# Relu² attention with a Fourier-mix feed-forward: mirrored rows stored by one indirect scatter, 112-row stores, DFT tables and first weights moved to the start

## The chip, the core and the metric

The kernel runs on one NeuronCore of a Trainium2 chip. TensorE (PE) does the matmuls and transposes, VectorE (DVE), ScalarE (ACT) and GpSimd (POOL) the elementwise work; PE's weight loads stand as PEld. SyncE (SP) issues the transfers that store and reload rows, and POOL those that load and cast the inputs. Each engine works through its own instructions in a fixed order; semaphores tie them together. The metric is device time in microseconds, lower is better.

## The reference

```python
# q, k, v: [8, 12, 448, 64] f32; w1: [768, 3072]; w2: [3072, 768]
scores = q @ k^T / 8
attn   = max(scores, 0)**2 / 448
x = heads joined: (attn @ v) -> [8, 448, 768]
mixed = real(fft(fft(x, axis=1), axis=2))
u  = x + mixed
un = (u - mean(u)) / sqrt(var(u) + 1e-6)         # over the last axis
out = u + max(un @ w1, 0) @ w2
```

## The kernel before

A pass runs once for each of the 8 batches, and three of them overlap. `attention(b)` makes for each pair of heads the scores (L374, PE), their relu (L406, ACT), its square (L400, DVE) and the product with v (L388, PE). `mix(b)` applies the two DFTs as matmuls with cosine and sine tables (`chan`, L555, and `seq`, L471), forms `u = x + mixed` and its normalised form `un` (L516, DVE), and turns `un` by PE (L598) into `unT`, which ACT copies out of PSUM (L602). `ffns` takes 384 tokens for an even batch and 512 for an odd one (its own 448 and the 64 left over), multiplies by w1 (L653), applies relu (L643, ACT), then for each chunk of 128 tokens and each half of the 768 columns multiplies by w2 (L688); DVE adds the product to the residual rows `o` (L670).

The DFT of a real sequence is symmetric, so `mix` computes tokens 0 to 224 and their mirror images 447 to 225 from the same products. It does so in two row pieces `ch`, and each makes two tiles: `us[0]` with tokens s (added on DVE, L491 and L492) and `us[1]` with tokens 448 - s (added on POOL, same lines). The residual rows wait in DRAM: `mix_store` writes `us[0]` to `usc` (L527), writes `us[1]`, whose rows stand in reverse order, to a second DRAM buffer `ubo` (L534), and when that has landed copies `ubo` to `usc` with the rows reversed (L537). The pieces have 113 and 112 rows; the four stores have 113, 112, 112 and 111 rows, and the copies are written as 2 x 112 x 384 and 2 x 111 x 384. `reload` later brings 128 rows of `usc` into one of two tiles `o` (L634); the tile is free again when the store of the finished chunk (L675) has landed.

All of L527, L534, L537, L634 and L675 are issued by SP, one after the other, and each may wait for a semaphore first. All input loads (q, k and v of a group of four heads, L252; w1 in two halves, L266; w2, L276) are issued by POOL and share its queue. The order is made by a planner in the kernel: generators yield the engine, a duration and what must be done first, and `Streams.run` emits the step that can start earliest; ties go by rank. `loading` lists the loads: batch 0, first half of w1, batch 1, second half of w1, w2, batch 2 and on. `build_dft` makes the tables: index rows by POOL (iota), angles on DVE (dfty and dftr, L195 to L231), sines on ACT (L199).

Of the kernel before, what the change touches and what calls it, by code (L numbers as in the profile page):

```python
# [9 lines left out]
FP32 = mybir.dt.float32  # L10
BF16 = mybir.dt.bfloat16
AF = mybir.ActivationFunctionType
ALU = mybir.AluOpType
# [101 lines left out]
def kernel(  # L115
# [9 lines left out]
    nc = tc.nc  # L125
# [10 lines left out]
    KN = D // 2 + 1  # L136
    HG = 4
    NG = H // HG
    SC = [(0, R1), (R1, NS)]
    XB = 2  # L140

    const = ctx.enter_context(tc.tile_pool(name="const", bufs=1))
# [2 lines left out]
    psum = ctx.enter_context(tc.psum_pool(name="ps", bufs=1))  # L145
    dram = ctx.enter_context(tc.tile_pool(name="dr", bufs=1, space=bass.MemoryType.DRAM))

    usc = dram.tile([B * S, D], FP32, name="usc")
    ubo = dram.tile([B * S, D], FP32, name="ubo")

    def psS():
        return psum.tile([128, 2, 512], FP32, name="psS", tag="S", bufs=2)
# [14 lines left out]
    eps_t = const.tile([128, 1], FP32, name="eps_t")  # L167
    ident = const.tile([128, 128], BF16, name="ident")

    rev = const.tile([128, R1], BF16, name="rev")  # L170
    qT_bufs = []

    def constants():
        make_identity(nc, ident)
        nc.gpsimd.memset(zero_t, 0.0)
        nc.gpsimd.memset(eps_t, 1e-6)
        for i in range(3):
            t = const.tile([128, NQ], BF16, name=f"qT{i}")
            nc.gpsimd.memset(t[:, NS:NS + 1], 0.0)
            nc.gpsimd.memset(t[:, NQ - 1:NQ], 0.0)  # L180
            qT_bufs.append(t)
        nc.gpsimd.memset(rev, 0.0)
        nc.gpsimd.affine_select(out=rev, in_=rev, compare_op=ALU.not_equal, fill=1.0, base=-R,
                                pattern=[[1, R1]], channel_multiplier=1)

    seq = const.tile([R1, 2, 2, NS], BF16, name="seqm")
    chan = [const.tile([128, 2, 2 * KH], BF16, name=f"chan{m}") for m in range(3)]
    dft_ready = Cell()

    def build_dft():  # L190
        def sincos(dst, y, n, p):

            e = yield need("DVE", n / 1920 + n / 960 + 0.3)
            r = work.tile([128, 4 * KH], FP32, name="dftr", tag="o", bufs=2)
            nc.vector.tensor_scalar(r[:p, :n], y[:p, :n], float(2 ** 23), float(2 ** 23),  # L195
                                    op0=ALU.add, op1=ALU.subtract)
            nc.vector.tensor_tensor(y[:p, :n], y[:p, :n], r[:p, :n], op=ALU.subtract)
            e = yield need("ACT", act(n), [e + LATENCY["DVE"]])
            nc.scalar.activation(dst, y[:p, :n], AF.Sin, bias=zero_t[:p], scale=2.0 * math.pi)  # L199
            dft_ready.t = e + LATENCY["ACT"]  # L200

        e = yield need("POOL", 1.4)
        row = const.tile([128, 8], FP32, name="drow")
        col = work.tile([128, 2 * KH], FP32, name="dcol", tag="tm", bufs=1)
        col2 = work.tile([128, 2 * KH], FP32, name="dcol2", tag="tp", bufs=1)
        nc.gpsimd.iota(row[:, 0:2], pattern=[[R1, 2]], base=0, channel_multiplier=1,
                       allow_small_or_imprecise_dtypes=True)
        nc.gpsimd.iota(row[:, 4:7], pattern=[[128, 3]], base=0, channel_multiplier=1,
                       allow_small_or_imprecise_dtypes=True)
        nc.gpsimd.iota(col[:, 0:NS], pattern=[[1, NS]], base=0, channel_multiplier=0,  # L210
                       allow_small_or_imprecise_dtypes=True)
        nc.gpsimd.iota(col2, pattern=[[1, 2], [2, KH]], base=0, channel_multiplier=0,
                       allow_small_or_imprecise_dtypes=True)
        e = yield need("DVE", 0.16, [e + LATENCY["POOL"]])
# [30 lines left out]
    def load_group(i):  # L245

        b, g = divmod(i, NG)
        hs = slice(g * HG, (g + 1) * HG)
        for x, (nm, src) in enumerate((("q", q), ("k", k), ("v", v))):
            e = yield need("POOL", 0.85, bufs=[BQ[x]])  # L250
            t = work.tile([R, 2 * HG, 2 * Dh], BF16, name=f"{nm}n", tag=f"{nm}n", bufs=3)
            nc.gpsimd.dma_start(  # L252
                out=t, in_=src[b, hs].rearrange("h (f p j) d -> p (h f) (j d)", f=2, j=2))
            loads[i][x] = t.rearrange("p (h f) (j d) -> p (f j) h d", f=2, j=2)
            ready[i][x].t = sch.dma(e, GRP)

    w1_sb = [[None] * 2 for _ in range(MC)]
    w2_sb = [None] * 4
# [22 lines left out]
    def loading():  # L281
        for i in range(NG):
            yield from load_group(i)
        yield from load_w1(0)
        for i in range(NG, 2 * NG):
            yield from load_group(i)
        yield from load_w1(1)
        yield from load_w2()
        for i in range(2 * NG, B * NG):
            yield from load_group(i)  # L290
# [231 lines left out]
    def mix_store(b, ch, us, ut, freed):  # L522
        s0, s1 = SC[ch]
        n = s1 - s0
        r0 = b * S
        e = yield need("SP", 0.1, [ut[0]])
        nc.sync.dma_start(out=usc[r0 + s0:r0 + s1, :], in_=us[0][:n])  # L527
        st0 = sch.dma(e, n * D * 4)
        u_stored[b][2 * ch].t = st0

        lo, hi = (1, R1) if ch == 0 else (0, n - 1)
        t0 = r0 + S - s0 - (hi - 1)
        e = yield need("SP", 0.1, [ut[1]])
        nc.sync.dma_start(out=ubo[t0:t0 + hi - lo, :], in_=us[1][lo:hi])  # L534
        st1 = sch.dma(e, n * D * 4)
        e = yield need("SP", 0.1, [st1] + freed)
        nc.sync.dma_start(  # L537
            out=usc[t0:t0 + hi - lo, :].rearrange("t (a d) -> a t d", a=2)[:, ::-1, :],
            in_=ubo[t0:t0 + hi - lo, :].rearrange("t (a d) -> a t d", a=2))
        u_stored[b][2 * ch + 1].t = sch.dma(e, n * D * 4)  # L540
        BU[0].free.append(max(st0, freed[0].t))
        BU[1].free.append(max(st1, freed[1].t))

    def mix(b):
# [44 lines left out]
        for m2 in range(3):  # L589
            e1 = yield need("PE", 8 * 0.06, un_ready[b], [BS])  # L590
            pu = psS()
            for h in range(2):
                ms = slice((2 * m2 + h) * 128, (2 * m2 + h + 1) * 128)
                for t, n, idn, c0, w in ((0, R1, ident[:R1, :R1], 0, R1),
                                         (2, R, ident[:R, :R], R1, R),
                                         (3, R, rev[:R, 2:R1], NS, R - 1),
                                         (1, R1, rev[:R1, 0:R], NS + R - 1, R)):
                    nc.tensor.matmul(pu[:, h, c0:c0 + w], lhsT=uns[b][t][:n, ms], rhs=idn,  # L598
                                     start=True, stop=True)
# [17 lines left out]
    def ffns():  # L617
        for b in range(B):
# [9 lines left out]
            def reload():  # L628
                c = len(os)
                if c < NC:  # L630
                    stored = u_stored[b] + (u_stored[b - 1] if b % 2 else [])
                    e = yield need("SP", 0.1, stored, [BO])
                    o = work.tile([128, D], FP32, name="o", tag="o", bufs=2)
                    nc.sync.dma_start(out=o, in_=usc[T0 + c * 128:T0 + (c + 1) * 128, :])  # L634
                    os.append((o, sch.dma(e, 128 * D * 4)))

            pend = None
# [60 lines left out]

    LEAD = 1.6
    with tc.manual_schedule():  # L700
        constants()
        sch.engine.update(POOL=1.8)

        sch.add(loading(), (0, 4))
        sch.add(build_dft(), (0, 9))
        sch.add(turning(), (2, 2))
        sch.add(ffns(), (4, 0))
        sch.add(mixes(), (1, 1))
# [32 lines left out]
```

## Time and profile before

| | |
|---|---|
| median of 3 runs | 796.37 us (796.13 to 797.03) |
| the profiled execution | 797.58 us; its span from first to last instruction 795.8 us |
| PE busy | 668.2 us, 84% of the span |
| DVE, ACT, POOL busy | 385.7, 357.6, 105.7 us |
| chain that ended last: waits on `o<-usc` and on `out_dram<-o` | 12% and 7% of the span |
| stores and mirror copies of the residual rows | 16 + 16 + 16 transfers of 333 to 339 KB |

All rows used below are of that one execution. A row of the timeline gives start, duration, engine, line, operation and tiles; the bracket at its end gives how long the engine had been idle and what it had waited for. A row of the windows gives, for one stretch, each engine's busy time with its count of instructions, then the granted TensorE clock (1.00 is full), the mean busy share of the 16 DMA engines, and GB/s. Line numbers are those of the kernel before; the changed kernel's own lines are named where its order is shown.

### The profile page before, as it was taken

To read this page: it belongs to the slowest core of one execution; us is meant where nothing else is said; L and a number is where in the kernel's file an instruction comes from. 1 tells how busy PE (TensorE), PEld (TensorE's weight loads), DVE (VectorE), ACT (ScalarE), POOL (GpSimd) and SP (SyncE) were. 2 spreads that over 40 slices of the span, in tenths; PEclk is the share of its full clock that TensorE was granted. 3 is DMA by queue.
4 is the path that set the end of the run, shared out by engine and by line. 5 is a ranking of instruction groups with operands and counts; after the bars stand their busy time and mean duration, and the time that the engine had idled before them with its cause. 6 is when DMAs were issued, how large, how long until landed. Compare 5 with 4: busy or idle time off the path is not lost.

```text
span 795.8 us, 10685 instructions
## 1 busy us (share of the span) xinstructions
PE 668.2 (84%) x4270; PEld 361.1 (45%) x4288; DVE 385.7 (48%) x894; ACT 357.6 (45%) x557; POOL 105.7 (13%) x144
## 2 busy tenths in 40 slices
PE   4774905996999769996999769996999779996998
PEld 2232402563446435563446444563446444563454
DVE  3987503484445635375454735375454644370001
ACT  3773713533664236533665136534565146522410
POOL 7134101120112111120112111120111100020000
PEclk9997766997999889997999988998999989998999
DMA  9959922622634255322634253332631232012212
GB/s 142 139 59 210 226 50 63 68 66 75 119 35 56 80 127 103 33 71 75 119 36 55 76 129 90 36 66 88 122 39 22 71 114 70 1 50 95 80 40 79
DMA packets 86114, 65.15 MB, mean 82 GB/s; under 512 B 67136, under 2 KB 73776, under 8 KB 86064
## 3 DMA queue, kind: packets, MB, share of 16 engines
q0 software_dynamic: 70528, 25.96, 27.6%
q1 hardware_dynamic: 15536, 38.52, 14.2%
q8 instruction: 33, 0.54, 0.3%
q14 instruction: 17, 0.14, 0.1%
HBM read 68.40 MB, written 27.50 MB: 121 GB/s over the span
## 4 chain that ended last, share of the span: by engine, by line
PE 55%; DMA 20%; DVE 13%; another core or an unknown queue 4%; ACT 3%; issue 2%; POOL 2%; SPq 0%; DVEq 0%; ACTq 0%; POOLq 0%
PE psF L653 28%; DMA o<-usc 12%; PE psF L688 11%; DMA out_dram<-o 7%; PE psT L388 5%; PE psS L374 4%; DVE sq L400 2%; PE psT L325 2%; PE psS L555 2%; DVE stats L502 2%; ACT rsc L406 1%; DVE o L670 1%; DMA w<-in_moe_w_ch_dram 1%; DVE un L516 1%
## 5 line engine op out<-in xcount | busy, mean ns | idle before, releaser
L406 ACT ACTIVATE rsc<-psS 112x900 bf16<-112x900 f32 x192 | 174.4, 920 | 216.4 <-DVE sq L400 122.1
L653 PE MATMUL psF<-unT,w 128*128 128x384 bf16 (+1 forms) x1134 | 236.8, 359 | 2.3 <-ACT hT L643 0.7
L688 PE MATMUL psF<-w,hT 128*128 128x384 bf16 x1344 | 237.8, 332 | 0.0
L688 PEld LDWEIGHTS <-hT 128*128 128x128 bf16 x1344 | 128.9, 99 | 95.8 <-issue 19.7
L653 PEld LDWEIGHTS <-w 128*128 128x128 bf16 x1152 | 109.0, 99 | 118.4 <-issue 30.7
L643 ACT ACTIVATE hT<-psF 128x384 bf16<-128x384 f32 (+1 forms) x192 | 104.3, 545 | 67.3 <-PE psF L653 67.0
L400 DVE TENSOR_TENSOR sq<-rsc 112x900 bf16<-112x900 bf16 x192 | 114.3, 620 | 40.7 <-ACT rsc L406 33.3
L670 DVE TENSOR_TENSOR o<-psF,o 128x384 f32<-128x384 f32 x56 | 30.7, 548 | 151.3 <-DMA o<-usc 82.2
L374 PE MATMUL psS<-qT,kT 64*112 64x450 bf16 x384 | 71.5, 433 | 15.0 <-ACT rsc L406 7.3
L252 POOL DMA_DIRECT2D vn<-in_v_dram x24 | 19.9, 828 | 415.5 <-PE psT L388 405.0
L388 PE MATMUL psT<-sq,vn 112*64 112x450 bf16 x384 | 65.9, 413 | 5.2 <-DVE sq L400 4.3
L414 DVE TENSOR_SCALAR xT<-psT 128x450 bf16<-128x450 f32 x48 | 30.0, 624 | 81.3 <-PE psT L388 81.1
L325 PE MATMUL psT<-ident,qkr 112*128 112x112 bf16 x336 | 28.9, 240 | 45.3 <-DVE xT L414 43.7
L325 PEld LDWEIGHTS <-qkr 112*128 112x128 bf16 x384 | 28.5, 116 | 64.0 <-DVE qkr L315 34.1
L598 PE MATMUL psS<-ident,un 113*128 113x113 bf16 x96 | 16.9, 283 | 36.2 <-ACT rsc L406 36.2
L374 PEld LDWEIGHTS <-kT 64*112 64x112 bf16 x384 | 23.1, 137 | 53.1 <-issue 45.8
L332 DVE COPY qT<-psT 128x224 bf16<-128x224 bf16 x42 | 16.4, 391 | 49.5 <-PE psT L325 49.3
L598 PEld LDWEIGHTS <-un 113*128 113x128 bf16 x192 | 17.8, 138 | 47.7 <-DVE qkr L315 37.5
L388 PEld LDWEIGHTS <-vn 112*64 112x64 bf16 x384 | 17.2, 114 | 43.3 <-issue 42.8
L491 POOL TENSOR_TENSOR u<-tp,xn 113x385 f32<-113x385 f32 (+1 forms) x16 | 14.9, 929 | 158.8 <-issue 96.0
L502 DVE BATCH_NORM_STATS2 stats<-u 113x6 f32<-113x384 f32 (+1 forms) x64 | 31.7, 535 | 0.7 <-POOL u L491 0.4
L602 ACT ACTIVATE unT<-psS 128x768 bf16<-128x768 f32 (+1 forms) x24 | 20.5, 868 | 20.3 <-PE psS L598 20.3
(71 smaller groups left out, 478.8 us busy)
## 6 DMA issues: line engine op xcount, KB each, us to landing
o<-usc SPq DMA_DIRECT2D x28, 384.0 KB
out_dram<-o SPq DMA_DIRECT2D x28, 384.0 KB
qn<-in_q_dram POOLq DMA_DIRECT2D x24, 224.0 KB, 5.5
kn<-in_k_dram POOLq DMA_DIRECT2D x24, 224.0 KB, 5.9
vn<-in_v_dram POOLq DMA_DIRECT2D x24, 224.0 KB, 4.4
w<-in_moe_w_ch_dram POOLq DMA_DIRECT2D x12, 384.0 KB, 11.4
w<-in_moe_w_ch_dram POOLq DMA_DIRECT2D x4, 1152.0 KB, 38.9
usc<-u SPq DMA_DIRECT2D x8, 339.0 KB
```

The lines of the kernel that those rows point to most:

```text
L325: nc.tensor.transpose(pt[:, x * S + c * R:x * S + (c + 1) * R], qk[x][:, c, hs], ident[:R, :R])
L374: nc.tensor.matmul(sc[:R, h, 0:NQ], lhsT=kT[ps, c * R:(c + 1) * R], rhs=qT[ps, :], start=True, stop=True)
L388: nc.tensor.matmul(av[h * Dh:(h + 1) * Dh, 0:NQ], lhsT=vn[:, c, h0 + h, :], rhs=sq[:, h, :], start=(c == 0), stop=(c == 3))
L400: nc.vector.tensor_tensor(sq, r, r, op=ALU.mult)
L406: nc.scalar.activation(r, sc[:R, :, 0:NQ], AF.Relu)
L414: nc.vector.tensor_scalar(x, av[:, 0:NQ], 1.0 / (64.0 * S), None, op0=ALU.mult)
L502: nc.vector.bn_stats(stats[:n, hf, :], u[:n, hf * (D // 2):(hf + 1) * (D // 2)])
L598: nc.tensor.matmul(pu[:, h, c0:c0 + w], lhsT=uns[b][t][:n, ms], rhs=idn, start=True, stop=True)
L643: nc.scalar.activation(h[:, 0:N], ph[:, 0:N], AF.Relu)
L653: nc.tensor.matmul(ph[:, 0:N], lhsT=w1_sb[m][hf][:, jj * 128:(jj + 1) * 128], rhs=unT[:, m, 0:N], start=(m == 0), stop=(m == MC - 1))
L670: nc.vector.tensor_tensor(o[:, hs], pc[:, 0:D // 2], o[:, hs], op=ALU.add)
L688: nc.tensor.matmul(pc[:, 0:D // 2], lhsT=hT[j][:, c * 128:(c + 1) * 128], rhs=w2_sb[j // 6][:, j % 6, hs], start=(j == 0), stop=(j == JC - 1))
```

## The change

1. The DRAM buffers `usc` and `ubo` become two tensors for each batch, `utop` (224 rows) and `ubot` (225 rows). The row pieces become 112 and 113 rows. SP stores 112 rows of `us[0]` for each piece, and for the second piece the one row left over goes to `ubot`. `us[1]` is written to `ubot` by one indirect DMA on POOL's queue: a column of row numbers (`back`) gives each partition its destination row, so the rows land already reversed. The copies of L537 and the buffer between are gone. A reload that crosses a tensor's border becomes two or three transfers.
2. The index rows for the DFT tables, `ident` and `rev` are made by POOL between the first loads, small memsets go to DVE, and `build_dft` gets the rank (0, 3) for (0, 9).
3. The second half of w1 is loaded before batch 1; w2 comes after batch 1.

```diff
-    SC = [(0, R1), (R1, NS)]
+    SC = [(0, R), (R, NS)]
-    usc = dram.tile([B * S, D], FP32, name="usc")
-    ubo = dram.tile([B * S, D], FP32, name="ubo")
+    HS = S // 2
+    utop = [dram.tile([HS, D], FP32, name=f"utop{b}") for b in range(B)]
+    ubot = [dram.tile([HS + 1, D], FP32, name=f"ubot{b}") for b in range(B)]
...
+        for i in range(2):
+            nc.gpsimd.iota(back[i], pattern=[[0, 1]], base=(2 - i) * R, channel_multiplier=-1)
...
+            if i == 0 and x == 1:
+                e = yield need("POOL", 1.0)
+                dft_indices()
+                indices_ready.t = e + LATENCY["POOL"]
...
         yield from load_w1(0)
+        yield from load_w1(1)
         for i in range(NG, 2 * NG):
             yield from load_group(i)
-        yield from load_w1(1)
         yield from load_w2()
...
         e = yield need("SP", 0.1, [ut[0]])
-        nc.sync.dma_start(out=usc[r0 + s0:r0 + s1, :], in_=us[0][:n])
+        nc.sync.dma_start(out=utop[b][s0:s0 + R, :], in_=us[0][:R])
+        if ch == 1:
+            nc.sync.dma_start(out=ubot[b][0:1, :], in_=us[0][R:R1])
...
-        e = yield need("SP", 0.1, [ut[1]])
-        nc.sync.dma_start(out=ubo[t0:t0 + hi - lo, :], in_=us[1][lo:hi])
+        e = yield need("POOL", 1.2, [ut[1]])
+        nc.gpsimd.indirect_dma_start(
+            out=ubot[b], out_offset=bass.IndirectOffsetOnAxis(ap=back[ch], axis=0),
+            in_=us[1][:R], in_offset=None)
-        e = yield need("SP", 0.1, [st1] + freed)
-        nc.sync.dma_start(
-            out=usc[t0:t0 + hi - lo, :].rearrange("t (a d) -> a t d", a=2)[:, ::-1, :],
-            in_=ubo[t0:t0 + hi - lo, :].rearrange("t (a d) -> a t d", a=2))
...
-        sch.add(build_dft(), (0, 9))
+        sch.add(build_dft(), (0, 3))
```

What SP issues around the mix of batch 2, while the second feed-forward group runs; before, `u` rows go out by four stores and two copies:

```order
L527 DMA usc_69<-u_2519 113x768
L534 DMA ubo_70<-u_2516 112x768
L634 DMA o_2535<-usc_69 128x768
L537 DMA usc_69<-ubo_70 2x112x384
L527 DMA usc_69<-u_2604 112x768
L534 DMA ubo_70<-u_2586 111x768
L675 DMA out_0_dram<-o_2157 128x768
L634 DMA o_2649<-usc_69 128x768
L537 DMA usc_69<-ubo_70 2x111x384
```

Now the same place on SP; the one-row store L548 waits until the first piece's scatter has landed, because both write `ubot`, and the second piece's scatter (L553, on POOL) waits in turn for that row:

```order
L546 DMA utop2_71<-u_2537 112x768
L658 DMA o_2553<-utop1_70 32x768
L658 DMA o_2553<-ubot1_78 96x768
L546 DMA utop2_71<-u_2623 112x768
L548 DMA ubot2_79<-u_2623 1x768
L700 DMA out_0_dram<-o_2175 128x768
L658 DMA o_2668<-ubot1_78 128x768
L700 DMA out_0_dram<-o_2553 128x768
```

The two copies and the two stores to `ubo` have left SP's row; the reload of the last chunk (o_2668) is behind one chunk store alone.

The loads in POOL's row, before, from the third group of batch 1 to the first piece of w2 (`w1_m_h` is row block m, half h):

```order
L252 DMA qn_469<-in_q_dram 112x8x128
L252 DMA kn_476<-in_k_dram 112x8x128
L252 DMA vn_588<-in_v_dram 112x8x128
L266 DMA w1_0_1_595<-in_moe_w_ch1_dram 128x1536
L266 DMA w1_1_1_597<-in_moe_w_ch1_dram 128x1536
L266 DMA w1_2_1_612<-in_moe_w_ch1_dram 128x1536
L266 DMA w1_3_1_635<-in_moe_w_ch1_dram 128x1536
L266 DMA w1_4_1_642<-in_moe_w_ch1_dram 128x1536
L266 DMA w1_5_1_659<-in_moe_w_ch1_dram 128x1536
L276 DMA w2_0_674<-in_moe_w_ch2_dram 128x6x768
```

And now, from the end of w1 to the first piece of w2:

```order
L286 DMA w1_4_1_278<-in_moe_w_ch1_dram 128x1536
L286 DMA w1_5_1_280<-in_moe_w_ch1_dram 128x1536
L262 DMA qn_296<-in_q_dram 112x8x128
L262 DMA kn_305<-in_k_dram 112x8x128
L262 DMA vn_380<-in_v_dram 112x8x128
L262 DMA qn_393<-in_q_dram 112x8x128
L262 DMA kn_399<-in_k_dram 112x8x128
L262 DMA vn_499<-in_v_dram 112x8x128
L262 DMA qn_506<-in_q_dram 112x8x128
L262 DMA kn_511<-in_k_dram 112x8x128
L262 DMA vn_618<-in_v_dram 112x8x128
L296 DMA w2_0_625<-in_moe_w_ch2_dram 128x6x768
```

All twelve pieces of w1 now stand ahead of batch 1's nine loads, where six of them stood behind these.

DVE's first instructions before go straight to the copies of q and k; the tables came in between the squares from the 26th instruction on. Now two tables' angles stand around the first copies:

```order
L225 TENSOR_SCALAR drow_91<-drow_91 128x2
L226 TENSOR_SCALAR drow_91<-drow_91 128x3
L232 TENSOR_SCALAR dfty_123<-dcol_92,drow_91 113x225 x2
L216 TENSOR_SCALAR dftr_130<-dfty_123 113x450
L218 TENSOR_TENSOR dfty_123<-dfty_123,dftr_130 113x450
L335 COPY qkr_135<-qn_111 112x1024
L232 TENSOR_SCALAR dfty_138<-dcol_92,drow_91 113x225 x2
L335 COPY qkr_143<-kn_113 112x1024
L216 TENSOR_SCALAR dftr_145<-dfty_138 113x450
L218 TENSOR_TENSOR dfty_138<-dfty_138,dftr_145 113x450
```

The work on the tables moved from the middle of batch 0's attention to its start; PE's own order changes by a few swaps in batch 0 alone.

More of the change, by code (lines that the diff above doesn't have):

```diff
@@ L168 @@
     ident = const.tile([128, 128], BF16, name="ident")
-    rev = const.tile([128, R1], BF16, name="rev")
+    rev = const.tile([128, R], BF16, name="rev")
+    back = [const.tile([R, 1], mybir.dt.int32, name=f"back{i}") for i in range(2)]
     qT_bufs = []
[L173 to L176, printed above, removed]
+    drow = const.tile([128, 8], FP32, name="drow")
+    dcol = work.tile([128, 2 * KH], FP32, name="dcol", tag="tm", bufs=1)
@@ new lines, with dft_indices @@
+    dcol2 = work.tile([128, 2 * KH], FP32, name="dcol2", tag="tp", bufs=1)
+    def dft_indices():
+        nc.gpsimd.iota(drow[:, 0:2], pattern=[[R, 2]], base=0, channel_multiplier=1,
+                       allow_small_or_imprecise_dtypes=True)
+        nc.gpsimd.iota(drow[:, 4:7], pattern=[[128, 3]], base=0, channel_multiplier=1,
+                       allow_small_or_imprecise_dtypes=True)
+        nc.gpsimd.iota(dcol[:, 0:NS], pattern=[[1, NS]], base=0, channel_multiplier=0,
+                       allow_small_or_imprecise_dtypes=True)
+        nc.gpsimd.iota(dcol2, pattern=[[1, 2], [2, KH]], base=0, channel_multiplier=0,
+                       allow_small_or_imprecise_dtypes=True)
@@ L177, in constants, with small_constants, mirrors @@
+    def small_constants():
+        nc.vector.memset(zero_t, 0.0)
+        nc.vector.memset(eps_t, 1e-6)
         for i in range(3):
             t = const.tile([128, NQ], BF16, name=f"qT{i}")
-            nc.gpsimd.memset(t[:, NS:NS + 1], 0.0)
-            nc.gpsimd.memset(t[:, NQ - 1:NQ], 0.0)
+            nc.vector.memset(t[:, NS:NS + 1], 0.0)
+            nc.vector.memset(t[:, NQ - 1:NQ], 0.0)
             qT_bufs.append(t)
+    def mirrors():
         nc.gpsimd.memset(rev, 0.0)
-        nc.gpsimd.affine_select(out=rev, in_=rev, compare_op=ALU.not_equal, fill=1.0, base=-R,
-                                pattern=[[1, R1]], channel_multiplier=1)
+        nc.gpsimd.affine_select(out=rev, in_=rev, compare_op=ALU.not_equal, fill=1.0,
+                                base=1 - R, pattern=[[1, R]], channel_multiplier=1)
+        for i in range(2):
+            nc.gpsimd.iota(back[i], pattern=[[0, 1]], base=(2 - i) * R, channel_multiplier=-1)
@@ L186 @@
     seq = const.tile([R1, 2, 2, NS], BF16, name="seqm")
     chan = [const.tile([128, 2, 2 * KH], BF16, name=f"chan{m}") for m in range(3)]
-    dft_ready = Cell()
+    dft_ready, indices_ready = Cell(), Cell()
     def build_dft():
@@ L200, in sincos @@
             dft_ready.t = e + LATENCY["ACT"]
[L202 to L214, printed above, removed]
+        row, col, col2 = drow, dcol, dcol2
+        e = yield need("DVE", 0.16, [indices_ready])
         nc.vector.tensor_scalar(row[:, 0:2], row[:, 0:2], 1.0 / S, None, op0=ALU.mult)
@@ L255, in load_group @@
             ready[i][x].t = sch.dma(e, GRP)
+            if i == 0 and x == 1:
+                e = yield need("POOL", 1.0)
+                dft_indices()
+                indices_ready.t = e + LATENCY["POOL"]
+            if i == 0 and x == 2:
+                yield need("POOL", 0.7)
+                make_identity(nc, ident)
+            if i == 1 and x == 2:
+                yield need("POOL", 0.7)
+                mirrors()
     w1_sb = [[None] * 2 for _ in range(MC)]
@@ L524, in mix_store @@
         n = s1 - s0
-        r0 = b * S
         e = yield need("SP", 0.1, [ut[0]])
-        nc.sync.dma_start(out=usc[r0 + s0:r0 + s1, :], in_=us[0][:n])
+        nc.sync.dma_start(out=utop[b][s0:s0 + R, :], in_=us[0][:R])
+        if ch == 1:
+            nc.sync.dma_start(out=ubot[b][0:1, :], in_=us[0][R:R1])
         st0 = sch.dma(e, n * D * 4)
         u_stored[b][2 * ch].t = st0
-        lo, hi = (1, R1) if ch == 0 else (0, n - 1)
-        t0 = r0 + S - s0 - (hi - 1)
-        e = yield need("SP", 0.1, [ut[1]])
-        nc.sync.dma_start(out=ubo[t0:t0 + hi - lo, :], in_=us[1][lo:hi])
+        e = yield need("POOL", 1.2, [ut[1]])
+        nc.gpsimd.indirect_dma_start(
+            out=ubot[b], out_offset=bass.IndirectOffsetOnAxis(ap=back[ch], axis=0),
+            in_=us[1][:R], in_offset=None)
         st1 = sch.dma(e, n * D * 4)
-        e = yield need("SP", 0.1, [st1] + freed)
-        nc.sync.dma_start(
-            out=usc[t0:t0 + hi - lo, :].rearrange("t (a d) -> a t d", a=2)[:, ::-1, :],
-            in_=ubo[t0:t0 + hi - lo, :].rearrange("t (a d) -> a t d", a=2))
-        u_stored[b][2 * ch + 1].t = sch.dma(e, n * D * 4)
+        u_stored[b][2 * ch + 1].t = st1
+        e = yield need("SP", 0.0, freed)
         BU[0].free.append(max(st0, freed[0].t))
@@ L593, in mix @@
                 ms = slice((2 * m2 + h) * 128, (2 * m2 + h + 1) * 128)
[L594 to L597, printed above, removed]
+                for t, n, idn, c0, w in ((0, R, ident[:R, :R], 0, R),
+                                         (2, R1, ident[:R1, :R1], R, R1),
+                                         (3, R, rev[:R, :], NS, R),
+                                         (1, R, rev[:R, 0:R - 1], NS + R, R - 1)):
                     nc.tensor.matmul(pu[:, h, c0:c0 + w], lhsT=uns[b][t][:n, ms], rhs=idn,
@@ L633, in reload @@
                     o = work.tile([128, D], FP32, name="o", tag="o", bufs=2)
-                    nc.sync.dma_start(out=o, in_=usc[T0 + c * 128:T0 + (c + 1) * 128, :])
+                    r0, end = T0 + c * 128, T0 + (c + 1) * 128
+                    t = r0
+                    while t < end:
+                        bb, r = divmod(t, S)
+                        src, r = (utop[bb], r) if r < HS else (ubot[bb], r - HS)
+                        w = min(HS - r, end - t)
+                        nc.sync.dma_start(out=o[t - r0:t - r0 + w, :], in_=src[r:r + w, :])
+                        t += w
                     os.append((o, sch.dma(e, 128 * D * 4)))
@@ L700 @@
     with tc.manual_schedule():
-        constants()
-        sch.engine.update(POOL=1.8)
+        small_constants()
+        sch.engine.update(POOL=0.5, DVE=0.8)
         sch.add(loading(), (0, 4))
-        sch.add(build_dft(), (0, 9))
+        sch.add(build_dft(), (0, 3))
         sch.add(turning(), (2, 2))
```

## The prediction

> **What bounds the kernel now.** I read the page's slices first, then the waits, then the timeline at the longest waits, then windows over them for the DMA engines and the clock.
>
> ```profile
> span 795.8 us, 10685 instructions
> PE   4774905996999769996999769996999779996998
> PEclk9997766997999889997999988998999989998999
> ```
>
> PE is at 9 in most slices; one early slice reads 0, and every few slices there is a dip to 6 or 7, each time with a lower clock. The waits from 130 us to the end (time, times, longest) name what PE and DVE stood for:
>
> ```profile
> DVE o L670 <- DMA o<-usc: 82.2, 10, 12.9
> PE psS L598 <- ACT rsc L406: 35.6, 6, 6.4
> PE psT L325 <- DVE xT L414: 17.0, 3, 6.4
> PE psS L598 <- DVE un L516: 7.5, 1, 7.5
> ```
>
> Ten waits of DVE for a reload, and 6 + 3 + 1 = 10 waits of PE, 35.6 + 17.0 + 7.5 = 60.1 us. They are the same ten places. Two of them, on DVE and PE, and SP's issues around them:
>
> ```profile
> 274.02 0.56 DVE L670 TENSOR_TENSOR o<-psF,o 128x384 f32<-128x384 f32 x1 [5.77 <-DMA o<-usc]
> 276.79 0.35 PE L598 MATMUL psS<-ident,un 113*128 113x113 bf16 x2 [5.46 <-ACT rsc L406]
> 293.30 0.56 DVE L670 TENSOR_TENSOR o<-psF,o 128x384 f32<-128x384 f32 x1 [12.39 <-DMA o<-usc]
> 295.52 0.90 PE L325 MATMUL psT<-ident,qkr 112*128 112x112 bf16 x8 [6.12 <-DVE xT L414]
> ```
>
> ```profile
> 254.18 0.34 SPq L675 DMA_DIRECT2D out_dram<-o  x1
> 256.30 0.24 SPq L527 DMA_DIRECT2D usc<-u  x1
> 256.59 4.57 SPq L534 DMA_DIRECT2D ubo<-u  x1
> 261.26 0.82 SPq L634 DMA_DIRECT2D o<-usc  x1
> 272.98 0.59 SPq L537 DMA_DIRECT2D usc<-ubo  x1
> ...
> 275.89 2.11 SPq L675 DMA_DIRECT2D out_dram<-o  x1
> 288.70 0.34 SPq L634 DMA_DIRECT2D o<-usc  x1
> ```
>
> The reload issued at 261.26 reached DVE only at 274.02, and the chunk store of 275.89 let its buffer go only at 288.70, 12.8 us each. DVE stands at its add, the squares and `un` queue behind it, then ACT and PE. Why 12.8 us for 384 KB is in the windows (last columns: clock, DMA share, GB/s):
>
> ```profile
> 354.00:357.50 3.50, 3.50 (x23) 2.07 (x22) 3.50 (x7) 0.54 (x1) 0.97 (x1) 1.00 0.74 218
> 357.50:366.00 8.50, 6.67 (x43) 3.57 (x41) 2.55 (x7) 1.59 (x3) 0.00 (x0) 1.00 0.07 29
> ```
>
> Most of a reload and of a 112-row store passes at 218 GB/s; then 29 GB/s at a share of 0.07 go on for 8.5 us. One engine of sixteen is 0.0625. A transfer of 113 rows, issued just ahead, takes 113 x 3 KB at 29 GB/s = 12 us if one engine carries it all, and what is queued behind it on that engine waits. So the dips are one busy DMA engine, not bandwidth.
>
> The early hole has the same sign:
>
> ```profile
> 101.34 13.79 SPq L537 DMA_DIRECT2D usc<-ubo  x2
> 121.50 0.43 DVE L315 COPY qkr<-qn 112x1024 bf16<-112x1024 bf16 x1 [23.16 <-DMA qn<-in_q_dram]
> 127.85 0.91 PE L325 MATMUL psT<-ident,qkr 112*128 112x112 bf16 x8 [26.70 <-DVE xT L414]
> 104.00:127.00 23.00, 0.00 (x0) 0.10 (x1) 0.60 (x2) 0.00 (x0) 0.00 (x0) 0.55 0.16 41
> ```
>
> PE stands 26.70 us for a load of batch 1 while the DMA engines are 0.16 busy: two or three of sixteen, shared with SP's mirror copies (2 x 112 x 384).
>
> **The change part by part.** *Stores of 112 rows, no copies.* All stores of the new kernel but the single row have 112 rows, the shape that passed at 218 GB/s above; 113, 111 and 2 x 112 are gone. A chunk store and a reload then cost a plain landing each. Their own price is hidden in this trace by the jam; the nearest rows are POOL's loads of 224 KB:
>
> ```profile
> L252 POOL DMA_DIRECT2D vn<-in_v_dram x24 | 19.9, 828 | 415.5 <-PE psT L388 405.0 <-PE psS L374 10.5
> DMA to landing us min/median/max: 3.7/5.4/59.4
> ```
>
> Store plus reload at two medians is 10.8 us. Room: the store of 254.18 and DVE at its add at 274.02 - 5.77 = 268.25, 14 us; the second add would come at 293.30 - 12.39 = 280.91 for a chunk store that follows 264 or so once SP is free, 16 us. So the ten waits go: -60.1 us, and at worst some return (rivals).
>
> Is something else late next? The tightest place is in the odd groups:
>
> ```profile
> 362.05 2.12 PE L688 MATMUL psF<-w,hT 128*128 128x384 bf16 x12
> 366.87 0.56 DVE L670 TENSOR_TENSOR o<-psF,o 128x384 f32<-128x384 f32 x1 [6.75 <-DMA o<-usc]
> ```
>
> DVE would go on at 366.87 - 6.75 = 360.12; L598 came 3.75 us after DVE's add (370.62, next fence), so at 363.87, and PE's matmuls end at 364.17. That is 0.3 us of room, and at 276.79 likewise: 271.02 against 271.33. Nothing is left over, but nothing is late.
>
> *The clock after each wait.* From the end of each wait to the record of full clock:
>
> ```profile
> 276.79:280.53 3.74, 3.74 (x29) 2.94 (x29) 3.13 (x10) 3.04 (x6) 0.00 (x0) 0.50 0.42 150
> 370.62:379.51 8.89, 8.23 (x47) 4.79 (x48) 4.68 (x12) 5.80 (x8) 0.00 (x0) 0.50 0.27 102
> 127.85:133.75 5.90, 5.90 (x27) 2.56 (x27) 3.33 (x9) 2.11 (x3) 0.00 (x0) 0.50 0.08 21
> sum 56.00, PE 53.95 PEld 31.65 DVE 32.72 ACT 35.65 POOL 0.00; mean PE 5.39 PEld 3.16 DVE 3.27 ACT 3.57 POOL 0.00
> ```
>
> The sum row is over the ten stretches that follow the ten waits: 56.0 us at half clock, 28.0 us lost. Three of them are like 370.62, where ACT is 5.80 of 8.89 busy and hands PE its `unT`; there I count only half of the 4 us as PE's own, so 28.0 - 3 x 2 = 22.0. The Trainium skill ("TensorE: Matmul & The Clock Gate", Part 1) says that full clock returns after about 3.4 us of busy time; by that, ten waits would cost 10 x 1.7 = 17 us and the sum below would end 5 us higher. The rows show half clock for 3.74 to 8.89 us, so the rows decide.
>
> *The early hole.* The copies are gone, and batch 1's loads stand ahead of w2: -26.7, and half of the 5.90 above, -2.95. The cover of the new order is the time until DVE first asks for batch 1:
>
> ```profile
> 51.98 0.42 DVE L315 COPY qkr<-qn 112x1024 bf16<-112x1024 bf16 x1
> 5.87:14.40 8.53, 3.48 (x28) 2.40 (x28) 3.40 (x11) 3.21 (x5) 6.42 (x10) 1.00 1.68 164
> 21.86:48.00 26.14, 19.59 (x88) 8.30 (x87) 25.23 (x64) 19.38 (x24) 4.92 (x6) 1.00 0.93 114
> 21.86:48.00 26.14, 10.24 (x20) 4.16 (x5) 1.00 0.93 114
> ```
>
> Ahead of it stand 9 loads of 224 KB and 12 of 384 KB, 6.8 MB, 41 us at 164 GB/s, so about 46 us with its own landing; the copy at 51.98 moves to about 48. Two microseconds of cover at the slowest rate; if it is gone, DVE waits as long as the load is late.
>
> *Tables at the start.* The last row is the tables' share alone (DVE, then ACT): DVE is busy 25.23 of 26.14 us there, 10.24 of it for tables, so this stretch is DVE's. Before 14.40 DVE idles 5.87 + 8.53 - 3.40 = 11.0 us, but the index rows now come after two load issues, so some 3.6 us of it pass first: 7.4 us can hide tables, the rest still stands ahead of the squares, and ACT's 4.16 us of sines now delay the first relus. Between 0 and -7.4 I take -3.5, the middle.
>
> *Scatter and single row.* POOL and its queue are where the new work goes:
>
> ```profile
> 254.70 1.15 POOL L492 TENSOR_TENSOR u<-tm,xn 113x383 f32<-113x383 f32 x1
> 260.09 0.92 POOL L491 TENSOR_TENSOR u<-tp,xn 112x385 f32<-112x385 f32 x1 [4.23 <-issue]
> ```
>
> No scatter is in the trace. Bounds: 0.83 us on POOL like a load, or more; between the two pieces POOL has 4.23 us. I take 1 us: 16 of them, all in idle time, 0 on the path. Landing at the loads' 5.4 puts the first scatter down at 255.85 + 1 + 5.4 = 262.3; SP reaches the one-row store after DVE's second `u`, about 263.5, so it doesn't wait; behind it on SP are chunk stores and the last reload. The second scatter lands near 274, and its rows are asked for in the next group, after 300. In batch 0 the scatter queues behind w2, and SP with it, but the first reload is 20 us later. The reloads' extra issues, 0.34 us each, are on idle SP: 0.
>
> Sum against the profiled 797.6 us (span 795.8 and 1.8 around it): 60.1 + 22.0 + 26.7 + 2.95 + 3.5 = 115.2, so 682.4. The median of the runs is 1.2 us below the profiled execution: 681.
>
> **The rivals.**
> - *The next link is late.* With 0.3 us of room, anything that slows DVE by 1 to 2 us in each mix (POOL's scatter beside it) brings back 10 x 1.5 = 15 us: 696. That is priced without a drop of the clock. For it: DVE has no gap there. Against: no row slows it.
> - *Part of the jam stays.* SP's row now waits for POOL at the one-row store; if scatters land 5 us later than I think, chunk stores and reloads are late and the clock drops again: 2 us in ten places and the 22 us of the clock, 723. Against: 14 to 16 us of room.
> - *The weights block batch 1.* If w1 lands 10 us late for it, 691. For: POOL's queue is served in order. Against: 2 us of cover even at the slow rate.
> - *The other side: the scatter holds POOL.* If one takes X us of POOL, the second `u` of each of 8 batches comes X - 4.23 later, and DVE, ACT and PE with it. The gains are eaten at 115/8 = 14.4, so X = 18.6 us, 22 times a load's issue. At 25 us: 681 + 8 x 20.8 = 847. Nothing in the trace speaks for it but that it is unknown.
> - *112 rows don't spread from these tiles*: the ten waits stay, 797 - 33 = 764. The window at 218 GB/s speaks against it.
>
> **How the numbers follow.** My forecast 0.66, with a range of its own of 668 (clock and tables gain all they can, 6 + 4, and a little more) to 690; next link late 0.17; part of the jam 0.08; weights 0.05; POOL held 0.02; no spread 0.02. The range 664 to 704 holds the forecast, the next link and the weights, and leaves out what is past 704 and the tails. About 0.2% is what a measurement of this kernel tells from no change, 1.6 us. Only the scatter rival is slower: faster 0.97, same 0.01, slower 0.02.
>
> **What the new profile would show.** Right: no wait of DVE for a reload over 1 us, PE at 9 from about 90 us on with no clock below 9, no stretch of 25 to 30 GB/s at a share of 0.06, the hole at 100 us gone, batch 0's last square about 3 us earlier. Wrong: DVE waiting for `o`, the one-row store waiting for its scatter, POOL's scatter over 4 us, or DVE waiting for q before 60 us.

## The result, and the profile after

The changed kernel takes 688.69 us (686.08 to 689.21, 4 runs) where the kernel before, beside it, takes 796.7 us (796.13 to 798.5): a ratio of 0.8634, with an interval of 0.8608 to 0.866. The forecast was 681 us with a range of 664 to 704, so the time lies inside, 7.7 us later than forecast.

The page of the changed kernel, same lines as before (the execution took 688.54 us):

```profile
span 686.8 us, 10715 instructions
PE   2777399999999999999999999999999999999997
PEclk9999589999999999999999999999999999999999
```

The dips to 6 and 7 are gone, and so are all drops of the clock behind the sixth slice. One stretch of 560 us, from 120 to 680 us, says the same in a row: first before, then after (columns: stretch, length, busy time of PE, PEld, DVE, ACT, POOL, then clock, DMA share, GB/s).

```profile
120.00:680.00 560.00, 496.15 (x3263) 267.65 (x3279) 290.60 (x670) 267.56 (x423) 66.44 (x77) 0.93 0.37 75
```

```profile
120.00:680.00 560.00, 554.36 (x3754) 303.85 (x3770) 303.06 (x693) 283.92 (x451) 84.39 (x92) 1.00 0.36 74
```

PE stood 64 us of these 560 before and stands 5.6 us now, at full clock, while the DMA engines move as many bytes a second. The waits of PE from 120 us to the end were 60.1 us in ten places; what is left of them now is one line of 1.9 us and two shorter ones:

```profile
PE psS L394 <- ACT unT L620: 1.9, 6, 0.4
PE psF L678 <- ACT hT L668: 1.4, 3, 0.7
PE psS L616 <- ACT unT L620: 0.7, 3, 0.2
```

Of the 109.0 us that the span lost (795.8 to 686.8), 27.5 are PE's busy time (668.2 to 640.7, the work being the same, so they are half clock) and 81.5 its idle time. SP's row in the mix of batch 2, and the windows over it:

```profile
220.41 0.33 SPq L546 DMA_DIRECT2D utop<-u  x1
220.83 0.38 SPq L658 DMA_DIRECT2D o<-utop  x1
221.26 0.49 SPq L658 DMA_DIRECT2D o<-ubot  x1
227.62 0.30 SPq L546 DMA_DIRECT2D utop<-u  x1
227.97 0.29 SPq L548 DMA_DIRECT2D ubot<-u  x1
228.62 0.36 SPq L700 DMA_DIRECT2D out_dram<-o  x1
231.38 0.34 SPq L658 DMA_DIRECT2D o<-ubot  x1
```

```profile
219.00:222.00 3.00, 3.00 (x21) 1.79 (x19) 2.96 (x7) 0.00 (x0) 1.99 (x2) 1.00 0.63 204
222.00:225.00 3.00, 3.00 (x21) 1.56 (x21) 2.90 (x8) 0.30 (x1) 0.78 (x1) 1.00 0.87 250
225.00:228.00 3.00, 3.00 (x21) 1.62 (x18) 3.00 (x5) 0.00 (x0) 1.24 (x2) 1.00 0.12 43
228.00:231.00 3.00, 3.00 (x20) 1.82 (x19) 2.93 (x9) 0.99 (x2) 0.00 (x0) 1.00 0.70 247
```

From the chunk store (228.62) to the reload that waits for its landing (231.38) it is now 2.8 us, where 12.8 stood in the kernel before. The bytes come in bursts of 200 to 250 GB/s; the low row is the gap before the store of 227.62, and no 8.5 us at 29 GB/s stand behind any of them.

### The profile page after: what moved, and what is told of

Same layout as the page of the kernel before. It is cut to its first block, busy times and chain, and to the rows that moved or that the text cites. A ratio compares the mean times of both kernels' runs of the same rounds, so it can differ in the third digit from the quotient of the medians.

```text
span 686.8 us, 10715 instructions
## 1 busy us (share of the span) xinstructions
PE 640.7 (93%) x4270; PEld 347.9 (51%) x4288; DVE 388.1 (57%) x902; ACT 354.9 (52%) x556; POOL 126.3 (18%) x154
## 3 DMA queue, kind: packets, MB, share of 16 engines
q1 hardware_dynamic: 10320, 27.56, 12.1%
## 4 chain that ended last, share of the span: by engine, by line
PE 67%; DVE 19%; ACT 5%; DMA 4%; issue 2%; POOL 2%; ACTq 0%; DVEq 0%; POOLq 0%
PE psF L678 32%; PE psF L713 18%; PE psT L408 5%; PE psS L394 5%; DVE stats L522 4%; ACT rsc L426 3%; DVE un L536 3%; PE psS L573 3%; DVE sq L420 2%; DVE o L695 2%; PE psT L345 2%; DMA kn<-in_k_dram 2%; DMA w<-in_moe_w_ch_dram 2%; DVE u L512 2%; PE psT L478 1%
## 5 line engine op out<-in xcount | busy, mean ns | idle before, releaser
L678 PE MATMUL psF<-unT,w 128*128 128x384 bf16 (+1 forms) x1134 | 231.5, 354 | 2.5 <-ACT hT L668 1.4
L713 PE MATMUL psF<-w,hT 128*128 128x384 bf16 x1344 | 231.6, 326 | 0.0
L394 PE MATMUL psS<-qT,kT 64*112 64x450 bf16 x384 | 67.6, 413 | 14.1 <-ACT rsc L426 7.3
L394 PEld LDWEIGHTS <-kT 64*112 64x112 bf16 x384 | 21.9, 132 | 50.3 <-issue 43.9
L511 POOL TENSOR_TENSOR u<-tp,xn 112x385 f32<-112x385 f32 (+1 forms) x16 | 14.9, 934 | 149.6 <-DVE tp L502 128.6
L345 PEld LDWEIGHTS <-qkr 112*128 112x128 bf16 x384 | 25.5, 107 | 18.0 <-DVE qkr L335 11.6
L522 DVE BATCH_NORM_STATS2 stats<-u 112x6 f32<-112x384 f32 (+1 forms) x64 | 31.6, 534 | 0.0
L526 ACT ACTIVATE std<-mv,eps_t 112x2 f32<-112x2 f32 (+1 forms) x16 | 4.7, 296 | 50.5 <-DVE mv L523 50.5
L536 DVE TENSOR_SCALAR un<-u,rstd,nmr 112x768 bf16<-112x768 f32 (+1 forms) x32 | 28.3, 915 | 0.6
L484 ACT ACTIVATE xn<-psT 112x768 bf16<-112x768 bf16 (+1 forms) x32 | 25.3, 812 | 6.5 <-PE psT L478 6.5
L586 DVE CAST pc<-psS 112x384 bf16<-112x384 f32 (+1 forms) x16 | 9.5, 594 | 32.0 <-ACT pc L584 32.0
```

The lines of the kernel that those rows point to most:

```text
L345: nc.tensor.transpose(pt[:, x * S + c * R:x * S + (c + 1) * R], qk[x][:, c, hs], ident[:R, :R])
L394: nc.tensor.matmul(sc[:R, h, 0:NQ], lhsT=kT[ps, c * R:(c + 1) * R], rhs=qT[ps, :], start=True, stop=True)
L522: nc.vector.bn_stats(stats[:n, hf, :], u[:n, hf * (D // 2):(hf + 1) * (D // 2)])
L536: nc.vector.tensor_scalar(un[:n], u[:n], rstd[:n, i:i + 1], nmr[:n, i:i + 1], op0=ALU.mult, op1=ALU.add)
L678: nc.tensor.matmul(ph[:, 0:N], lhsT=w1_sb[m][hf][:, jj * 128:(jj + 1) * 128], rhs=unT[:, m, 0:N], start=(m == 0), stop=(m == MC - 1))
L713: nc.tensor.matmul(pc[:, 0:D // 2], lhsT=hT[j][:, c * 128:(c + 1) * 128], rhs=w2_sb[j // 6][:, j % 6, hs], start=(j == 0), stop=(j == JC - 1))
```

## The experiments

The theory (A in the expectations): some transfers of the kernel before are carried by one, two or three of the sixteen DMA engines, because of their number of rows, and everything queued behind them on those engines waits. Rivals: the round trip through a second DRAM buffer and SP's waits for it; the order of the loads; the tables.

**Half of a mix's stores in an awkward shape.** In the changed kernel each store of 112 rows of `us[0]` is cut in two, at 109 rows, at 106, or at 96; nothing else changes.

```diff
-        nc.sync.dma_start(out=utop[b][s0:s0 + R, :], in_=us[0][:R])
+        for c0, c1 in ((0, 109), (109, R)):      # or (0, 106), (106, R); or (0, 96), (96, R)
+            nc.sync.dma_start(out=utop[b][s0 + c0:s0 + c1, :], in_=us[0][c0:c1])
```

> The changed kernel with each 112-row store of us[0] written as 109 rows and 3 rows: 109 has no divisor that could spread it. Nothing else changes. Theory A (such a transfer is carried by one engine, 109 x 3 KB at 29 GB/s = 11.5 us, and what is queued behind on that engine waits): the two stores of a mix hold one engine for 23 us, reloads and chunk stores behind them land late, DVE waits for o and PE with it 3 to 8 us a mix, 712 to 750 us; windows show a share of 0.07 at 29 GB/s for several us in each mix. Rival B (shapes do not matter): 688 to 690 us.

> The changed kernel with each 112-row store of us[0] as 106 + 6 rows (106 = 2 x 53). The one with 109 + 3 rows took 776.1. Theory A (the number of engines is the largest divisor up to 16 of the rows, here 2): 106 x 3 KB at 2 x 27 GB/s = 6 us for each in place of 12, so the two of a mix hold their engines for half as long; with the same stores behind them 690 to 735 us, and windows with a share near 0.13 and 50 to 60 GB/s. Rival B (any store that is not spread over all engines goes by one): 770 to 780 us. Rival C (it is the two transfers in place of one): 776 us as well.

> The changed kernel with each 112-row store of us[0] as 96 + 16 rows, both of them multiples of 16: as many transfers as with 109 + 3 or 106 + 6 rows. Theory A: all engines carry them, 688 to 690 us. Rival C (two transfers in place of one cost): 700 to 776 us.

A fourth kernel has 109 + 3 rows for the second piece alone (`ch == 1`), and 96 + 16 for the first:

> The changed kernel with the second piece's store alone as 109 + 3 rows, the first piece's as 96 + 16. Theory A: one engine is held for 12 us once in a mix; the chunk store and the reload behind it have some 9 us of room (the reload is asked for 16 us after the chunk store), so it costs 0 to 5 us a mix, 690 to 730 us, well under half of the 87 us that two of them cost. Rival D (each such store costs the same, 87 / 16 = 5.4 us): 732 us.

| rows of the two stores of a mix | median us | from the chunk store to the reload behind it, batch 2 |
|---|---|---|
| 96 + 16 and 96 + 16 | 686.64 (2 runs) | 226.57 to 229.12: 2.6 us |
| 106 + 6 and 106 + 6 | 693.44 (2 runs, 691.73 and 695.16) | 229.69 to 239.14: 9.5 us |
| 96 + 16 and 109 + 3 | 707.71 (2 runs) | 232.36 to 243.80: 11.4 us |
| 109 + 3 and 109 + 3 | 776.13 (4 runs) | 258.70 to 270.27: 11.6 us |

The rows of the table's last column, in the same order:

```profile
226.57 0.36 SPq L701 DMA_DIRECT2D out_dram<-o  x1
229.12 0.34 SPq L659 DMA_DIRECT2D o<-ubot  x1
```

```profile
229.69 0.36 SPq L701 DMA_DIRECT2D out_dram<-o  x1
239.14 0.34 SPq L659 DMA_DIRECT2D o<-ubot  x1
```

```profile
232.36 0.36 SPq L701 DMA_DIRECT2D out_dram<-o  x1
243.80 0.34 SPq L659 DMA_DIRECT2D o<-ubot  x1
```

```profile
246.12 11.59 SPq L547 DMA_DIRECT2D utop<-u  x2
257.81 0.85 SPq L549 DMA_DIRECT2D ubot<-u  x1
258.70 0.36 SPq L701 DMA_DIRECT2D out_dram<-o  x1
270.27 0.34 SPq L659 DMA_DIRECT2D o<-ubot  x1
```

The windows show how many engines were at work while a chunk store was waited for: behind the 106-row store, then behind the second 109-row store of the last kernel.

```profile
234.00:236.00 2.00, 2.00 (x15) 1.20 (x14) 2.00 (x6) 1.19 (x2) 0.00 (x0) 1.00 0.13 52
```

```profile
262.00:270.00 8.00, 8.00 (x53) 4.15 (x51) 1.22 (x3) 3.24 (x6) 0.00 (x0) 0.86 0.06 26
```

One engine of sixteen is a share of 0.0625, so 0.13 at 52 GB/s is what two engines give and 0.06 at 26 GB/s is what one gives. (A low share alone shows nothing, as the gap from 225 to 228 us in the result above; here a transfer was queued and waited for.) So the number of rows alone, with the same bytes and the same number of transfers, turns the new kernel back into one of 776 us. The rivals "shapes don't matter", "two transfers cost" and "what is not spread over all engines goes by one" are out. The control's 686.64 us lies a little under the 688 to 690 expected; the last section comes back to it. The Trainium skill ("DMA: Bandwidth & Descriptors", "Why a DMA increments its semaphore by 16 and not by 1") gives the rule: the number of engines is the largest one up to 16 that divides the slowest dimension of both sides, so 112 and 96 rows go by 16, 106 by 2, 113 and 109 by 1. The shares of 0.13 and 0.06 agree.

The expectation for 109 rows twice, 712 to 750 us, was too low, and the two cases don't add: one such store in a mix costs 21 us over the control (707.71 - 686.64), two cost 89.5. One store holds its engine for about 13 us (an estimate: 109 x 3 KB at 26 GB/s), which uses up the room of the chunk store and the reload. With two in a mix SP itself also stands, 11.59 us over the two issues of the second piece in the row above, and everything it would issue next is late by that too. With one it stands less, 4.62 us at the same place:

```profile
227.38 4.62 SPq L547 DMA_DIRECT2D utop<-u  x2
```

That the standing issue is what makes two such stores cost over four times as much as one fits these rows, but was not tried apart.

**The old path with good shapes.** The kernel before, with both DRAM buffers and the copies:

```diff
-        nc.sync.dma_start(out=usc[r0 + s0:r0 + s1, :], in_=us[0][:n])
+        for c0, c1 in ((0, R), (R, n)): ...               # 112 rows, and 1 if n is 113
-        nc.sync.dma_start(out=ubo[t0:t0 + hi - lo, :], in_=us[1][lo:hi])
+        ...                                               # 112 rows, or 96 and 15
-            out=usc[...].rearrange("t (a d) -> a t d", a=2)[:, ::-1, :],
+            out=usc[...].rearrange("t (a d) -> a t d", a=16)[:, ::-1, :],
```

> The kernel before with its round trip kept (stores to usc and ubo, mirror copies on SP, pieces of 113 and 112 rows, old loads and tables): only the shapes of the transfers change. A store of 113 rows becomes 112 + 1, one of 111 becomes 96 + 15, and the copies, 2 x 112 x 384 before, are written as 16 x 112 x 48. Theory A (the jam is transfers that few DMA engines carry, whatever their path): the ten waits, the half clock and the hole go, 684 to 700 us, and no stretch of 25 to 30 GB/s at a share of 0.06 is left. Rival B (the round trip itself costs: SP waiting for ubo, 5.4 MB more through DRAM): 740 to 797 us.

It takes 694.47 us (693.93 to 695.13; ratio 0.871, 0.8692 to 0.8728). So 102 of the change's 108 us are gained with the round trip, SP's waits, the load order and the tables all as they were. The shapes of stores and copies were changed together; what each is worth alone is not shown. Another form, with the copies as whole rows of 768 in reverse order, gave no time. From 120 us on PE is as busy as in the changed kernel:

```profile
120.00:680.00 560.00, 554.53 (x3763) 303.24 (x3780) 306.88 (x703) 290.13 (x461) 68.13 (x78) 1.00 0.43 83
```

What it lacks is in the early place, where DVE still waits for a load and the clock drops, but now with busy DMA engines (the copies go in packets of 48 numbers, 192 bytes; the share of 1.49 to 1.58 counts packets that overlap each by itself, so it can pass 1) where the share was 0.16 before:

```profile
103.66 0.43 DVE L315 COPY qkr<-qn 112x1024 bf16<-112x1024 bf16 x1 [4.95 <-DMA qn<-in_q_dram]
```

```profile
101.00:104.00 3.00, 0.52 (x4) 0.10 (x1) 0.34 (x1) 1.26 (x3) 0.00 (x0) 0.98 1.49 162
104.00:110.00 6.00, 1.91 (x12) 1.41 (x13) 2.44 (x9) 0.00 (x0) 0.00 (x0) 0.50 1.58 244
```

So the scatter and the missing round trip, together with whatever the small packets cost, are worth the 8.9 us to the stores-only kernel below. The price of the small packets alone was not measured.

**The parts apart.** Three kernels beside the changed one, run again as a yardstick on the same chip: its loads put back (batch 1 ahead of w1's second half), its tables put back, and both put back, which leaves the new stores alone. A fourth has the old stores with the new loads and tables.

```diff
-        yield from load_w1(1)
         for i in range(NG, 2 * NG):
             yield from load_group(i)
+        yield from load_w1(1)
```

```diff
-        sch.add(build_dft(), (0, 3))
+        sch.add(build_dft(), (0, 9))       # and constants() and the index rows as before
```

> The changed kernel once more, as the yardstick for the three kernels run beside it. All theories: 686 to 689 us. Its runs so far lay at 686.1 and at 688.5 to 689.2, so a second look also says how far apart two equal kernels may lie.

> The changed kernel with the second half of w1 loaded after batch 1 again. Theory A (the early hole of 26.7 us was made by DMA engines jammed with 113-row stores and mirror copies, not by the order of the loads; and the weights ahead of batch 1 now cost about 2.5 us, the waits of DVE at 41.98 and behind it): no hole comes back, 685 to 688 us, DVE waits under 1 us for batch 1's first q. Rival B (the order of the loads closed the hole, as the prediction had it): the hole comes back, 710 to 718 us.

> The changed kernel with the index rows, ident, rev and the DFT tables made as before (tables behind the squares). Theory A (tables at the start delay batch 0's first squares and slow the first instructions of DVE and POOL, so they cost): 683 to 686 us, first square of batch 0 back near 14.4 us. Rival B (the prediction's term, tables at the start save 3.5 us): 692 us.

> Part 1 of the change alone: 112-row stores, scatter, one-row store, no copies; loads in the old order, tables as before. Theory A (all the gain is in the stores; parts 2 and 3 cost 3.5 and 2.5 us): about 682 to 684 us, faster than the changed kernel, first mix matmul back near 59 us. Rival B (parts 2 and 3 gain 3.5 and 26.7 us as predicted): 715 to 720 us. Rival C (only the order of the loads pays): 714 us.

> The kernel before with its old stores and copies, but the loads in the new order and the tables at the start. Theory A (the jam makes the waits; batch 1's loads now come before the first mix stores, so the hole goes even with the jam; the startup costs 6 us): 797 - 26.7 - 3 + 6 = 773 us, the ten waits as before. Rival B (the waits of DVE come from late loads or tables as well): under 750 us. Rival C (the hole is made by the copies at any place of the loads): 797 to 803 us.

| stores | loads | tables | median us |
|---|---|---|---|
| new | new | at the start | 688.81 (687.36 to 690.08) |
| new | old | at the start | 687.07 (685.55 to 688.51) |
| new | new | late | 690.42 (690.18 to 691.48) |
| new | old | late | **685.57** (684.99 to 686.38) |
| old | new | at the start | 779.21 (778.25 to 781.95) |

The stores alone are the fastest version: a ratio of 0.8602 (0.8577 to 0.8627), better than both kernels. Parts 2 and 3 together cost 3.2 us, in runs that don't overlap here; of the changed kernel's four runs in the result, one (686.08) lies among those of the stores alone. The new order of the loads costs 4.9 us when the tables are late; when they are early, the 1.7 us lie within the spread of the runs. The tables at the start save 1.6 us with the new loads, in runs that just clear each other; with the old ones the runs overlap. So the expectation that each costs by itself (3.5 and 2.5) did not hold: for the tables with the new loads it had the wrong sign, and the 692 us of its rival B came nearer than the 683 to 686 expected. With the new stores in place, the prediction that both gain was wrong in sign for the pair. One way in which the two parts depend on each other is seen in POOL's row: with late tables the new loads stand ahead of the index rows too, which are made from 30.47 us on, and from 20.67 us on with the old loads.

With the old stores, parts 2 and 3 gain 17 us, fewer than the 24 expected. The ten waits of DVE stay, and the early hole only shrinks (PE waits 9.1 us there for 26.7); a wait of that kernel, and a window in its hole, with the DMA engines as idle as before:

```profile
DVE o L684 <- DMA o<-usc: 82.2, 10, 12.8
```

```profile
104.00:110.00 6.00, 0.00 (x0) 0.10 (x1) 0.15 (x1) 0.00 (x0) 0.00 (x0) 0.51 0.14 45
```

## Why the prediction came out as it did

**The ten waits and the clock behind them: right.** In the stores-only kernel, which has none of the startup changes, the span is 684.6 us: 111.2 less than before. The terms without the tables, 60.1 + 22.0 + 26.7 + 2.95, come to 111.75. The split was a little off. PE's busy time fell by 27.5 us (668.2 to 640.7) where 22.0 + 2.95 = 24.95 was taken, so less than half of the 3 x 2 us kept for ACT came back as well. Its idle time fell by 83.7 (127.6 to 43.9) for 86.8. That the sum meets to 0.6 us is luck in part: the two misses, 2.6 and 3.1 us, cancel.

**The 0.3 us of room: it held.** No add of DVE waits for a reload any more, and PE's waits for DVE in the mixes are gone from the list. The rival of the next link (696) did not happen.

**Scatter and single row: right.** A scatter stands 1.11 us on POOL in the mean (1 was taken), in time when POOL had nothing else. The one-row store waited for its scatter once, in batch 0, 12.1 us long, and POOL for the one-row store 49.5 us in 8 places; nobody waits behind.

```profile
L553 POOL DMA_INDIRECT ubot<-u,back x16 | 17.8, 1114 | 51.7 <-DMA ubot<-u 49.5 <-POOL u L512 2.0 <-DVE stats L522 0.3
```

```profile
SPq L548 <- DMA ubot<-u,back: 12.1, 1, 12.1
POOL ubot L553 <- DMA ubot<-u: 49.5, 8, 15.7
```

These are a group's row, then a wait of SP and one of POOL.

**The early hole: right size, half of the reason wrong.** The copy at 121.50 does not take a load of batch 1, as the prediction says. A batch has three groups; the copies of q before it, at 5.87, 11.50, 24.14, 39.22, 51.98 and 81.11, use up batches 0 and 1, and the seventh takes the first load of batch 2. That one is issued behind w2 in both kernels:

```profile
63.70 0.82 POOL L276 DMA_DIRECT2D w<-in_moe_w_ch_dram  x1 [1.48 <-DMA w<-in_moe_w_ch_dram]
65.53 0.83 POOL L252 DMA_DIRECT2D qn<-in_q_dram  x1 [1.00 <-DMA w<-in_moe_w_ch_dram]
```

So the place of batch 1's loads ahead of w2 gave it nothing. The new order helps it in another way: the second half of w1, issued here from 55.98 us on just ahead of w2, is out by 26.3 us in the changed kernel, and the load is issued at 61.39 us for 65.53. With the old stores and the new loads and tables it goes out at 60.73 us, and 9.1 of PE's 26.7 us of wait stay. With the new stores and the old order it goes out as late as before, at 66.26 us with late tables and 65.24 with early ones, and the hole is gone all the same (685.57 and 687.07 us). So the other half of the prediction's reason, the copies and stores that held the engines, is the one that closes the hole.

**The weights ahead of batch 1: the failed step.** The cover was counted to the copy at 51.98. By the same count that is batch 1's second; its first is at 39.22:

```profile
39.22 0.42 DVE L315 COPY qkr<-qn 112x1024 bf16<-112x1024 bf16 x1
```

In place of 2 us of cover there were some 7 us too few for a landing at 46. It landed at 42, and DVE waited, which the prediction names as a sign of being wrong (waiting for q before 60 us) and as the rival of the weights (which took 10 us late, and 691). The sum has nothing for it; the loads cost 4.9 us with late tables and 1.7, within the spread, with early ones. After, and then with the old loads and late tables:

```profile
41.98 0.43 DVE L335 COPY qkr<-qn 112x1024 bf16<-112x1024 bf16 x1 [3.14 <-DMA qn<-in_q_dram]
```

```profile
39.86 0.42 DVE L321 COPY qkr<-qn 112x1024 bf16<-112x1024 bf16 x1
```

**Tables at the start: the other failed term.** -3.5 was taken, between 0 and -7.4, and batch 0's last square was to come about 3 us earlier. It came 2.5 us later (55.15 us for 52.65), and the first instruction of a mix 2.6 us later (before, then after):

```profile
58.82 0.64 PE L555 MATMUL psS<-chan,fold 128*113 128x193 bf16 x3 [0.58 <-ACT rsc L406]
```

```profile
61.46 0.64 PE L573 MATMUL psS<-chan,fold 128*112 128x193 bf16 x3 [0.58 <-ACT rsc L426]
18.07 0.59 PE L408 MATMUL psT<-sq,vn 112*64 112x450 bf16 x2 [3.66 <-DVE sq L420]
3.46 0.80 DVE L225 TENSOR_SCALAR drow<-drow 128x2 f32<-128x2 f32 x1 [2.39 <-POOL drow L182]
```

The delay at the mix belongs to the loads, not to the tables. The same instruction with the new stores and the old loads, first with the tables at the start, then with late ones:

```profile
58.63 0.64 PE L573 MATMUL psS<-chan,fold 128*112 128x193 bf16 x3 [0.58 <-ACT rsc L426]
```

```profile
59.46 0.64 PE L559 MATMUL psS<-chan,fold 128*112 128x193 bf16 x3 [0.58 <-ACT rsc L412]
```

With the new loads and late tables it stands at 60.44 us. These are single executions, and two of the changed kernel differ by 0.5 us here (61.46 and 60.98). So with the old loads the tables at the start bring the mix forward by some 0.8 us, in place of 3.5, and the new loads put it back by 1 us with late tables and by over 2 with early ones. The idle time of DVE that was to take them was partly spent waiting for POOL's index rows (2.39 us), and they went ahead of the first squares: PE, which began its first products with v at 15.12 us before, now waits for a square until 18.07. In the time of the whole kernel they save 1.6 us with the new loads and cost 1.5 with the old ones, where the runs overlap; a gain of 3.5 shows in neither. What the pair costs, 3.2 us, in place of a gain of 3.5 makes 6.7 of the 7.7 us by which the forecast was short. The split between tables and loads is not settled to better than 2 us, since each depends on the other.

**The other rivals.** No part of the jam stayed (723), the scatter did not hold POOL (847), and 112 rows do spread (764): 2.8 us from the chunk store to its reload.

## What to carry to other kernels

Look at the DMA share in windows behind a late transfer: one sixteenth (0.06) or two (0.13), with everybody waiting, means a transfer that few engines carry, and giving the transfers shapes that spread (113 rows as 112 + 1, the copies over 16) may be worth more than removing the whole path around them (102 of 108 us here). Such jams don't add up in proportion: one a mix cost 21 us and two 89.5, with SP standing 11.6 us at its issues in the second case. When the cover of a moved load is counted, name the tile that each reader takes, not the line: here the same line's fifth and seventh instance were taken for others, and a change that rode along with a good one cost 3 us.

## What the runs showed of the hardware that was not expected

The granted clock changes on a grid. In the traces' own clock records, every stretch between two changes, in all twelve profiled runs, lasts a multiple of 3.413 us; only the last one of a record, which the record's end cuts off, does not. And the first stretch of half clock does not have one length for one kernel: the changed kernel had 20.48 us of it (6 steps) from 71.85 on in one execution and 23.89 us (7) from 69.06 on in another; the control with 96 + 16 rows had 13.65 us (4) from 73.74 on.

From the first matmul of batch 1's mix to the end, these three executions and the kernels with loads, tables or both put back all take 556.94 to 556.98 us. That matmul stands between 127.12 and 132.76 us, so the few us by which these kernels differ are decided ahead of it. The control's 2 us under the changed kernel are of this kind: its first mix instruction is at 61.46 us as well, and its half clock is two or three steps shorter. Why it is shorter there was not tried.

Early instructions of DVE can take several times their later time: the two smallest on the index rows took 0.80 and 0.72 us at 3.5 us, while POOL was making index rows and issuing loads, where the same two took 0.16 us in the kernel before. With late tables and the new loads, right behind POOL's index rows again, they took 0.38 and 0.29 us. What in POOL's work slows them was not tried apart.
